# Batch 0 of a fused RWKV, routed attention and MLP kernel: projected and scaled in two halves of three chunks, with the instruction order derived anew

## Chip, cores, metric

One Trainium2 chip, one core of it. The metric is device time in microseconds of one execution. Five engines matter: TensorE (PE in the rows; PEld is its weight load), VectorE (DVE), ScalarE (ACT), GpSimd (POOL) and SyncE (SP), which issues all DMA transfers.

## What is computed

The reference, cut to what matters (B=4 batches, H=8 heads, S=768 tokens, D=48, so 384 model columns; E=4 experts of width 64; hidden width 1536):

```
for t in range(S):                       # RWKV, per batch and head
    cur = einsum('bhd,bhe->bhde', u * k[t], v[t])
    y[t] = einsum('bhd,bhde->bhe', r[t], state + cur)
    state = w[t] * state + einsum('bhd,bhe->bhde', k[t], v[t])
x = y as [B, S, 384]
w = softmax of the top 2 of x @ w_gate   # per token
for e in range(E):                       # causal attention of each expert
    q, k, v = x @ wq[e], x @ wk[e], x @ wv[e]
    ye = softmax(causal(q k^T / 8)) @ v @ wo[e]
    out += (w of e where e is chosen) * ye
xn = layernorm(out) * g_ln
return out + relu(xn @ w1) @ w2
```

## The kernel before

A batch is 6 chunks of 128 tokens. `rwkv_chunk` (24 times) does the recurrence of a chunk with two scans on VectorE (L637 backward, L649 forward), masked products `pa` and `py` on TensorE, and adds the chunk's 384 columns to the tile `xf` (`xsum`, L782); ScalarE's `xabs` (L786) leaves the sum of the absolute values of each row in `xm`.

`project(b)` waits for all six `xabs`, takes the largest row sum (L803), turns it into a power-of-two scale (`pow2_scale`, L395 to L428, with two hops over TensorE), and splits `xf` into a high and a low fp16 half (`xs`, L823 and L827). SyncE transposes each chunk (L836). TensorE makes queries and keys (`pq`, L858: four column blocks `mt`, each in two halves of three chunks) and values (`pv`, L913, one per chunk). Queries and keys go through ScalarE and VectorE (`qk`, L871, L877) and are stacked by 4 or 6 DMAs per `mt` into `qs`, `kd` and `low` (L894 to L897). The gate weights of all six chunks follow in `g_rank`, `g_exp`, `g_norm`.

`attend(b)` goes through 6 row blocks i and 4 experts e: scores `ps` (L1000 to L1002), their smallest negated value on VectorE (`s_max`, L1012), the exponential and its high half on ScalarE (L1020, L1029), the low half on VectorE (`s_lo`, L1034), a DMA transpose into `pt` (`s_tr`, L1042), then the product with the values, `po` (L1055). After four experts the block is normalized, transposed (L1096) and projected, `px` (L1107). Two blocks make a group: `norm` (its last VectorE step is `n_lo`, L1165, then a transpose, L1172) and `mlp`: 108 matmuls `pm` (L1200) and 72 `pz` (L1233). There are 12 groups.

The weights w1 and w2 are also loaded, repacked (L491 to L493), scaled and split in the kernel, in its first 200 us.

Every step is recorded as an operation with its engine, a cost, what it waits for and which buffers it takes and frees. `Plan.order` sorts the operations: of those that can start about now on an engine, the one with the smallest due number goes first. The due numbers come from the table `PLACE` (by group and by step). So the order of each engine is fixed when the program is built, and each engine works strictly in that order. Where the planner sees TensorE free before 208 us of its own count, it puts in a `spin` (L583), a matmul into a scratch bank whose result nobody reads.

At the end `f_rows` (L1328) makes a flag from bounds on the data; only if it fails is everything computed again by a general loop.

Of the kernel before, what the change touches and what calls it, by code (L numbers as in the profile page):

```python
# [9 lines left out]
F32 = mybir.dt.float32  # L10
# [280 lines left out]
def transpose_time(cols):  # L291
    return 1.2 + 0.05 + max(0, cols - 768) * 0.28e-3, (0.9, cols * 1.17e-3)


def copy_time(elems, n=1):
    return 0.43 * n, (0.43 * n + 0.45, P * elems * 4 / 360e3)
# [1119 lines left out]
```

## Time and profile before

| | us |
|---|---|
| median of 3 runs | 718.54 |
| lowest, highest | 717.99, 721.35 |
| the profiled execution | 721.46 |
| its span, first to last instruction | 719.3 |
| TensorE busy | 661.2 |
| VectorE busy | 518.3 |
| ScalarE busy | 397.0 |
| mean granted TensorE clock | 0.964 |

2.2 us of the profiled execution lie outside its span. TensorE's busy time includes the spins, which do nothing for the output. Busy times overlap between engines; what counts is which engine is the last to be ready in each stage.

### The profile page before, as it was taken

Reading aid. Unit: us, or ns where it says so; the run is one execution under the profiler, and the core shown is the slowest. Engines: PE = TensorE matmul, PEld = TensorE weight load, DVE = VectorE, ACT = ScalarE, POOL = GpSimd, SP = SyncE. Lnnn points to the kernel's source line nnn. Section 1 sums busy time; section 2 is a strip of 40 time slices with the busy share of each in tenths; the row PEclk is TensorE's granted clock in tenths of the full one; section 3 lists DMA queues with packets and bytes.
Section 4 is the critical chain, followed back from the end, with each engine's and each line's share of the span. In section 5 each row is a group of like instructions: output and inputs, shape, how many; then the busy total and the mean of one; then the engine's idle time right before and its main releaser. Section 6 shows DMA issues by size and latency. Waiting matters only on the chain.

```text
span 719.3 us, 15287 instructions
## 1 busy us (share of the span) xinstructions
PE 661.2 (92%) x5651; PEld 478.4 (67%) x5656; DVE 518.3 (72%) x1300; ACT 397.0 (55%) x1175; POOL 95.9 (13%) x118
## 2 busy tenths in 40 slices
PE   7799668998999999988999899999999899999996
PEld 4467325666686787767678777758676667776773
DVE  8889989988899887787889857755554566564321
ACT  4634387756766655546766554656552467554410
POOL 4311200221323122102032200000000000000000
PEclk9989769999999999998999999999999999999998
DMA  8365664665859867647759434575445335444210
GB/s 301 117 197 177 222 171 103 165 163 106 165 152 228 132 144 184 183 86 154 152 122 235 121 86 85 107 119 93 92 64 118 71 60 118 90 81 75 43 45 26
DMA packets 172275, 92.59 MB, mean 129 GB/s; under 512 B 144416, under 2 KB 156448, under 8 KB 172192
## 3 DMA queue, kind: packets, MB, share of 16 engines
q1 hardware_dynamic: 172192, 91.53, 56.1%
q8 instruction: 46, 0.75, 0.5%
q14 instruction: 37, 0.30, 0.1%
HBM read 44.31 MB, written 4.72 MB: 68 GB/s over the span
## 4 chain that ended last, share of the span: by engine, by line
PE 59%; DMA 20%; DVE 14%; issue 2%; ACT 2%; SPq 1%; POOL 1%; DVEq 0%; ACTq 0%; POOLq 0%
PE pz L1233 16%; DMA pt<-hl 14%; PE pm L1200 13%; PE pq L858 4%; PE py L753 4%; PE po L1055 4%; PE spin L583 3%; PE pv L913 3%; PE pa L713 3%; PE px L1107 2%; PE pd L762 2%; PE ps L1000 2%; DVE bw L637 2%; PE ps L1001 2%; DVE w_w L492 1%
## 5 line engine op out<-in xcount | busy, mean ns | idle before, releaser
L1200 PE MATMUL pm<-xnT,w_w 128*128 128x256 f16 x1296 | 155.5, 274 | 0.5 <-DVE hid L1215 0.3
L1233 PE MATMUL pz<-w_w,hid 128*128 128x384 f16 x864 | 151.8, 326 | 0.2
L1200 PEld LDWEIGHTS <-w_w 128*128 128x128 f16 x1296 | 124.1, 98 | 17.0 <-DVE hid L1215 1.0
L1233 PEld LDWEIGHTS <-hid 128*128 128x128 f16 x864 | 81.5, 98 | 49.1 <-issue 0.7
L1020 ACT ACTIVATE ps<-ps,bias,scales 128x512 f32<-128x512 f32 (+3 forms) x128 | 76.6, 599 | 62.8 <-DVE junk L1012 62.3
L583 PE MATMUL spin<-starts,ident 128*128 128x512 bf16 x293 | 79.3, 412 | 2.9 <-POOL ident masks.py:199 2.1
L1034 DVE SCALAR_TENSOR_TENSOR hl<-ps,hl 128x512 f16<-128x512 f32 (+3 forms) x128 | 60.4, 499 | 24.6 <-ACT hl L1029 24.2
L1012 DVE TENSOR_SCALAR_CACHE_REDUCE junk<-ps,scales 128x512 bf16<-128x512 f32 (+3 forms) x96 | 58.8, 613 | 24.0 <-PE ps L1002 12.2
L1215 DVE SCALAR_TENSOR_TENSOR hid<-pm,hid 128x512 f16<-128x512 f32 x72 | 49.3, 686 | 28.5 <-ACT hid L1211 28.4
L1211 ACT ACTIVATE hid<-pm 128x512 f16<-128x512 f32 x72 | 42.6, 593 | 45.2 <-PE pm L1200 44.9
L1055 PE MATMUL po<-vt,pt 128*128 128x64 f16 x1008 | 45.2, 194 | 20.8 <-DMA pt<-hl 20.4
L1029 ACT ACTIVATE hl<-ps 128x512 f16<-128x512 f32 (+3 forms) x128 | 52.8, 448 | 20.0 <-DMA pt<-hl 19.5
L1055 PEld LDWEIGHTS <-pt 128*128 128x128 f16 x1008 | 38.9, 99 | 35.2 <-DMA pt<-hl 30.9
L583 PEld LDWEIGHTS <-ident 128*128 128x128 bf16 x298 | 30.3, 105 | 38.1 <-issue 13.1
L858 PE MATMUL pq<-xT,w_qk 128*128 128x384 f16 x288 | 49.6, 326 | 0.6 <-DVE inv_w L420 0.5
L753 PE MATMUL py<-seq,am 128*128 128x48 f32 x384 | 47.7, 279 | 0.0
L753 PEld LDWEIGHTS py<-seq,am 128*128 128x128 f32 x384 | 46.9, 198 | 1.1 <-DVE w_w L492 0.2
L677 POOL TENSOR_TENSOR tok<-tok 128x384 f32<-128x384 f32 x24 | 24.7, 1027 | 149.0 <-DMA tok<-in_tok_dram 137.8
L1149 POOL TENSOR_TENSOR rs_y<-rs_v,half 128x2 f32<-128x2 f32 x12 | 9.1, 760 | 262.8 <-DVE rs_v L1145 262.7
L1000 PE MATMUL ps<-kd,qs 128*128 128x512 f16 (+3 forms) x128 | 39.3, 308 | 2.3 <-DVE hl L1034 2.0
L697 POOL TENSOR_TENSOR cv<-seq,cb 128x384 f32<-128x384 f32 x24 | 23.4, 976 | 130.7 <-ACT cv L786 45.9
L858 PEld LDWEIGHTS <-w_qk 128*128 128x128 f16 x288 | 27.8, 98 | 19.1 <-DVE lg L926 0.6
(183 smaller groups left out, 1092.5 us busy)
## 6 DMA issues: line engine op xcount, KB each, us to landing
seq<-in_seq_dram SPq DMA_DIRECT2D x48, 256.0 KB, 4.4
tok<-in_tok_dram SPq DMA_DIRECT2D x24, 384.0 KB, 3.7
w_raw<-in_w_dram SPq DMA_DIRECT2D x24, 384.0 KB, 4.0
seq<-in_seq_dram SPq DMA_DIRECT2D x24, 258.5 KB, 2.9
seq<-in_seq_dram SPq DMA_DIRECT2D x24, 192.0 KB, 4.6
out_dram<-x SPq DMA_DIRECT2D x24, 192.0 KB, 2.2
qs<-qk SPq DMA_DIRECT2D x32, 96.0 KB, 2.3
kd<-qk SPq DMA_DIRECT2D x32, 96.0 KB, 2.2
```

The source lines that it names most:

```text
L583: T.matmul(bank("m", "spin"), ident16, ballast, start=True, stop=True)
L753: T.matmul(t["py"][:, h * D : (h + 1) * D], ams[h % 2][:, h // 2, :], t["vt"][:, h * D : (h + 1) * D], start=(c == 0 and h == 0), stop=(h ...
L858: T.matmul(h["pq", half][:, :384].rearrange("p (c t) -> p c t", t=P), wt["qk"][:, lw, kk, mt * P : (mt + 1) * P], t["xT"][:, 3 * half : 3 ...
L1000: T.matmul(ps, q, t["kd"][:, e, k0:k1], start=True, stop=False)
L1012: V.tensor_scalar(junk[:, k0:k1], h["ps"][ip], t["nesc"], least[:, :1] if ip else 3.0e38, op0=OP.mult, op1=OP.min, accum_out=h["bias"])
L1020: A.activation(ps, ps, AF.Exp, bias=h["bias"], scale=t["esc"], accum_out=r["sums"][:, ip, e : e + 1])
L1029: A.activation(h["hl"][:, k0:k1], ps, AF.Copy, scale=2.0 ** 14)
L1034: V.scalar_tensor_tensor(out=h["hl"][:, W + k0 : W + k1], in0=ps, scalar=2.0 ** 14, in1=h["hl"][:, k0:k1], op0=OP.mult, op1=OP.subtract)
L1055: T.matmul(r["po"][:, e * HD : (e + 1) * HD], r["pt"][e][:, lp * (i + 1) + kb, :], t["vt"][:, kb, lv, e * HD : (e + 1) * HD], start=(e == ...
L1200: T.matmul(h["pm"][:, j * 256 : (j + 1) * 256].rearrange("p (c t) -> p c t", t=P), wt["w1"][:, 4 * kk + f // 3, lw, f % 3 * P : (f % 3 + 1 ...
L1215: V.scalar_tensor_tensor(out=hid[fp][:, 1], in0=h["pm"], scalar=0.0, in1=hid[fp][:, 0], op0=OP.max, op1=OP.subtract)
L1233: T.matmul(h["po"][:, :DM], hid[fp][:, lh, c0 : c0 + P], wt["w2"][:, 2 * fp + j, lw, :], start=(fp + j + i == 0), stop=(fp == NF // 2 - 1 ...
```

## The change

Six things, by the diff.

1. Batch 0 alone (`SPLIT = 1`) is projected in two parts, chunks 0 to 2 and 3 to 5. Its scale waits for three `xabs` and is taken from the first half with a target of 2^10 in place of 2^14. Each `x_hi` now also waits for its chunk's own sum.
2. In that batch `pq` is done half by half, and each half of an `mt` has its own buffer and its own 4 or 6 stacking DMAs, of 384 columns instead of 768: 40 DMAs instead of 20.
3. The scores of row blocks 0 to 2 of batch 0 wait only for the first four stacks and the first three values; the gate steps are done once per half.
4. The flag checks in addition that the second half stays below 2^15 times under that scale (three small VectorE steps).
5. Five small products of scales move from GpSimd to VectorE.
6. `PLACE` holds other numbers, the planner's costs of DMAs and of some steps are other, and the `pt` transposes of a batch must keep their recorded order. `junk`, which nobody reads, shrinks to 512 columns.

```diff
-    ('av', 0, 0): -11321.78, ('av', 0, 1): -5901.15, ('av', 0, 2): -17242.11, ('av', 0, 3): -12213.17,
+    ('av', 0, 0): -16394.28, ('av', 0, 1): -10556.83, ('av', 0, 2): -24769.79, ('av', 0, 3): -11565.63,
...
+SPLIT = 1
...
-    return 1.2 + 0.05 + max(0, cols - 768) * 0.28e-3, (0.9, cols * 1.17e-3)
+    return 1.2 + 0.05 + max(0, cols - 768) * 0.28e-3, (0.9, cols * 1.2e-3)
...
-    return 0.43 * n, (0.43 * n + 0.45, P * elems * 4 / 360e3)
+    return 0.43 * n, (0.43 * n + 0.92, P * elems * 4 / 335e3)
...
-    junk = const.tile([P, S], BF16, name="junk")
+    junk = const.tile([P, 512], BF16, name="junk")
...
-        G.tensor_tensor(out=t[:, 0:1], in0=inv[:, 0:1], in1=inv[:, 1:2], op=OP.mult)
+        V.tensor_tensor(out=t[:, 0:1], in0=inv[:, 0:1], in1=inv[:, 1:2], op=OP.mult)
...
-                G.tensor_scalar(wt["gs"], g_sb, s, None, op0=OP.mult)
+                V.tensor_scalar(wt["gs"], g_sb, s, None, op0=OP.mult)
...
+        split = b < SPLIT
+        parts = ((0, 1, 2), (3, 4, 5)) if split else (tuple(range(NC)),)
...
-            V.tensor_reduce(out=cm, in_=xf[b][1], axis=AX.X, op=OP.max)
+            V.tensor_reduce(out=cm, in_=xf[b][1][:, : len(parts[0])], axis=AX.X, op=OP.max)
...
-        scaled = pow2_scale(x_max, 1, 14, f"x{b}", x_scales, [chunk[NC * b + c]["xabs"] for c in range(NC) if b < B] + small_done[:1])
+        scaled = pow2_scale(x_max, 1, 10 if split else 14, f"x{b}", x_scales,
+                            [chunk[NC * b + c]["xabs"] for c in parts[0] if b < B] + small_done[:1])
...
-            @op("A", 0.61, after=[scaled], take=[("xs", (b, c))])
+            @op("A", 0.61, after=[scaled] + ([chunk[NC * b + c]["xsum"]] if split else []), take=[("xs", (b, c))])
...
-        for mt in range(4):
+        for mt, half in [(mt, half) for half in range(2) for mt in range(4)] if split else [(mt, half) for mt in range(4) for half in range(2)]:
...
+            hlk = ("hl", ("q", b, mt, half if split else 0))
+            first, last = split or half == 0, split or half == 1
...
-                    nc.sync.dma_start(dst[a, e, :], hi[a, :])
+                    nc.sync.dma_start(dst[a, e, cols], hi[a, :])
...
+        for some in parts:
+            gate, n, cs = {}, len(some), slice(some[0], some[-1] + 1)
...
-                @op("PE", (2 * W + P) / 2400 + 0.0025 * (2 * npc + 1), after=pr["stacks"], follow=[before_ps, pr["mv"][-1]], take=aks, free=final)
+                @op("PE", (2 * W + P) / 2400 + 0.0025 * (2 * npc + 1), after=pr["stacks"][:4] if pr["split"] and i < 3 else pr["stacks"], follow=[before_ps, pr["mv"][2 if pr["split"] and i < 3 else -1]], take=aks, free=final)
...
-                @op("SP", d, after=[s_lo], dma=lat, take=[("pt", key)], free=[("hl", key)])
+                @op("SP", d, after=[s_lo], follow=me["tr"][-1:], dma=lat, take=[("pt", key)], free=[("hl", key)])
...
+            V.tensor_reduce(out=ok[:, k], in_=xf[b][1][:, 3:], axis=AX.X, op=OP.max)
+            V.tensor_tensor(out=ok[:, k], in0=ok[:, k], in1=cur[b]["s"], op=OP.mult)
+            V.tensor_scalar(ok[:, 1:2], ok[:, k], 2.0 ** 15, ok[:, 1:2], op0=OP.is_le, op1=OP.mult)
```

What moves, at three places. First VectorE where batch 0's scale begins, with the row `xcm` (its reduction). `xf`'s row names the chunk by the middle number of `py_5` or `py_2`; `w_w` is the repacking of w1 and w2. Before:

```order
L782 TENSOR_TENSOR xf_315<-py_5_941,cv_5_1017 128x384
L420 TENSOR_SCALAR inv_w_1035<-sc_w_1019 128x1
L422 TENSOR_SCALAR inv_w_1035<-inv_w_1035 128x1
L423 TENSOR_SCALAR inv_w_1035<-inv_w_1035 128x1
L424 TENSOR_SCALAR inv_w_1035<-inv_w_1035 128x1
L428 RECIPROCAL s_w_1036<-inv_w_1035 128x1
L803 TENSOR_REDUCE xcm_1046<-xm_316 128x1
L491 TENSOR_SCALAR w_w_127<-w_raw_1003 128x384
```

and now:

```order
L786 TENSOR_TENSOR xf_319<-py_2_568,cv_2_618 128x384
L677 TENSOR_TENSOR rp_3_632<-seq_3_420,fw_3_614 128x512
L495 TENSOR_SCALAR w_w_126<-w_raw_474 128x384
...
L724 COPY_PREDICATED am_91<-above,pa_3_0_673 128x512
L724 COPY_PREDICATED am_92<-above,pa_3_1_674 128x512
L814 TENSOR_REDUCE xcm_704<-xm_320 128x1
L779 TENSOR_TENSOR dec_98<-dec_98,pd_3_696 48x4x48 x2
L641 SCALAR_TENSOR_TENSOR bw_4_716<-seq_4_625,starts 128x516
```

The scale's reduction stood behind chunk 5 and w1's scale; it now stands in chunk 3, before the scan of chunk 4.

Second TensorE at the first matmul of the first MLP group (`pm_0_0`). `ps_4_0` is the score of row block 4, expert 0; `pd_4` and `pa_4` belong to chunk 4 of batch 1. Before:

```order
L762 MATMUL pd_4_2523<-seq_4_2071,k2t_4_2506 112x96 x4
L1000 LDWEIGHTS qs_1439
L1000 MATMUL ps_4_0_0_2531<-kd_1566,qs_1439 128x512
L1001 LDWEIGHTS qs_1439
L1001 MATMUL ps_4_0_0_2531<-low,qs_1439 128x512
...
L1002 MATMUL ps_4_0_512_2532<-neg,ident_73 128x128
L1200 LDWEIGHTS w_w_126
L1200 MATMUL pm_0_0_2543<-xnT_0_2478,w_w_126 128x256
```

and now:

```order
L717 MATMUL pa_4_0_2414<-rp_4_2396,k_1_4_2345 128x128
L717 MATMUL pa_4_1_2415<-rp_4_2396,k_1_4_2345 128x128
L1027 LDWEIGHTS qs_1014
L1027 MATMUL ps_3_0_0_2436<-kd_1124,qs_1014 128x512
L1028 LDWEIGHTS qs_1014
L1028 MATMUL ps_3_0_0_2436<-low,qs_1014 128x512
L1029 LDWEIGHTS ident_73
L1029 MATMUL ps_3_0_0_2436<-neg,ident_73 128x128
L1228 LDWEIGHTS w_w_126
L1228 MATMUL pm_0_0_2444<-xnT_0_2371,w_w_126 128x256
```

The first MLP group used to start behind the first score of block 4; it now starts behind the first score of block 3, and three scores of block 3 and the `py` of chunk 4 come after it.

Third TensorE between the last score of row block 4 (`ps_4_3`) and the product that uses it (`po` with `pt_4_3`), in batch 0. Before:

```order
L1002 MATMUL ps_4_3_512_2943<-neg,ident_73 128x128
...
L1233 MATMUL pz_0_0_2927<-w_w_127,hid_0_3_2719 128x384
...
L1055 MATMUL po_4_2726<-vt_1213,pt_4_2_2940 128x64
...
L1233 MATMUL pz_0_1_3033<-w_w_127,hid_0_0_2603 128x384
...
L1002 MATMUL ps_5_0_512_3044<-neg,ident_73 128x128
...
L1233 MATMUL pz_0_1_3033<-w_w_127,hid_0_3_2719 128x384
...
L1055 MATMUL po_4_2726<-vt_1213,pt_4_3_3041 128x64
```

and now:

```order
L1029 MATMUL ps_4_3_512_2952<-neg,ident_73 128x128
...
L1261 MATMUL pz_0_1_2982<-w_w_127,hid_0_0_2489 128x384
...
L1083 MATMUL po_4_2788<-vt_914,pt_4_2_2949 128x64
...
L1029 MATMUL ps_5_0_512_3027<-neg,ident_73 128x128
...
L735 MATMUL pk_0_3057<-ident,k_2_0_3003 128x128 x4
...
L1261 MATMUL pz_0_1_2982<-w_w_127,hid_0_2_2589 128x384
...
L1083 MATMUL po_4_2788<-vt_914,pt_4_3_3024 128x64
```

Between the two stood 54 matmuls `pz`; now 18 `pz` and the `pa` and `pk` of one chunk stand there.

## Rows read from the trace of the kernel before

**Rows 1.** The page's first line: span and instructions.

```profile
span 719.3 us, 15287 instructions
```

**Rows 2.** Busy time by stage: start:end, length, PE, PEld, DVE, ACT, POOL, PEclk, DMA, GB/s.

```profile
0.00:192.90 192.90, 162.68 (x1094) 104.23 (x1100) 173.01 (x396) 112.13 (x373) 43.72 (x56) 0.90 0.64 173
192.90:224.00 31.10, 30.47 (x320) 26.12 (x321) 27.26 (x67) 20.43 (x64) 10.94 (x11) 1.00 0.64 170
224.00:282.00 58.00, 55.37 (x515) 41.22 (x514) 48.33 (x109) 36.06 (x115) 11.05 (x12) 1.00 0.79 164
```

**Rows 3.** Waits of TensorE from 200 us on: total us, times, longest.

```profile
PE po L1055 <- DMA pt<-hl: 18.1, 18, 2.5
```

**Rows 4.** Timeline at the first MLP group: start, us, instructions [idle before <-releaser].

```profile
193.79 0.96 DVE L1165 TENSOR_TENSOR x<-xn,x 128x768 f16<-128x768 f32 x1 [1.33 <-ACT x L1161]
...
198.51 1.70 PE L1200 MATMUL pm<-xnT,w_w 128*128 128x256 f16 x14 [0.18 <-DMA xnT<-x]
```

**Rows 5.** Groups by line on VectorE: count | busy us, mean ns | idle before.

```profile
L1012 DVE TENSOR_SCALAR_CACHE_REDUCE junk<-ps,scales 128x512 bf16<-128x512 f32 x48 | 35.8, 746 | 17.5 <-PE ps L1001 9.2 <-PE ps L1002 7.0
L720 DVE COPY_PREDICATED am<-above,pa 128x512 f32<-128x512 int8 x48 | 32.9, 721 | 1.4 <-PE pa L713 1.3
L1034 DVE SCALAR_TENSOR_TENSOR hl<-ps,hl 128x512 f16<-128x512 f32 x48 | 32.5, 682 | 14.0 <-ACT hl L1029 13.9
L637 DVE TENSOR_TENSOR_SCAN bw<-seq,starts 128x516 f32<-128x516 f32 x24 | 30.9, 1288 | 3.9 <-DMA seq<-in_seq_dram 3.9
L649 DVE TENSOR_TENSOR_SCAN fw<-seq,begin 128x516 f32<-128x516 f32 x24 | 30.4, 1268 | 0.0
L673 DVE TENSOR_TENSOR rp<-seq,fw 128x512 f32<-128x512 f32 x24 | 16.3, 680 | 0.0
L782 DVE TENSOR_TENSOR xf<-py,cv 128x384 f32<-128x384 f32 x24 | 13.1, 548 | 3.1 <-PE py L753 2.8
L924 DVE SCALAR_TENSOR_TENSOR vt<-pv,vt 128x256 f16<-128x256 f32 x24 | 10.1, 420 | 9.4 <-ACT vt L920 9.3
L926 DVE TENSOR_SCALAR lg<-pv,scales 128x4 f32<-128x4 f32 x24 | 5.1, 211 | 0.0
```

**Rows 6.** Pieces of the chain that ended last, 200 to 480 us: start, us, work.

```profile
204.06 1.06 PE py L744 x8
...
212.06 1.72 PE py L753 x16
...
214.75 1.09 PE pa L713 x16
...
220.36 0.84 PE pd L762 x8
...
346.05 0.35 PE po L1055 x12
```

**Rows 7.** Timeline from the last score of block 4 to the second group.

```profile
224.21 0.38 PE L1000 MATMUL ps<-kd,qs 128*128 128x512 f16 x1 [0.66 <-DVE hl L1034]
...
224.43 0.38 PE L1001 MATMUL ps<-low,qs 128*128 128x512 f16 x1
...
224.81 3.09 PE L1233 MATMUL pz<-w_w,hid 128*128 128x384 f16 x18
...
224.87 0.95 DVE L1165 TENSOR_TENSOR x<-xn,x 128x768 f16<-128x768 f32 x1
...
236.64 0.61 PE L1055 MATMUL po<-vt,pt 128*128 128x64 f16 x15 [0.98 <-DMA pt<-hl]
...
239.75 2.46 PE L1200 MATMUL pm<-xnT,w_w 128*128 128x256 f16 x21
```

**Rows 8.** DMA issues by line: count, KB each, median us to landing.

```profile
qs<-qk SPq DMA_DIRECT2D x32, 96.0 KB, 2.3
```

**Rows 9.** The stacking DMAs on SyncE: ns shortest/median/longest, first and last start.

```profile
L894 SPq DMA_DIRECT2D qs<-qk x16: 461/588/607, 125.3 to 549.0; - x16
```

**Rows 10.** Waits of SyncE's own queue, 60 to 200 us: total us, times, longest.

```profile
SPq L516 <- ACT w_raw L387: 23.7, 14, 4.7
```

More of the change, by code (lines that the diff above doesn't have):

```diff
@@ L96 @@
+    'q_lo': -1695.12, 's_exp': 4159.27, 's_hi': -8021.02, 's_lo': -1628.8, 's_max': -1264.05, 's_tr': -7263.35,
+    'scan': -1954.79, 'se': 777.16, 'stack': -456.7, 'state': 1790.61, 'times': 1101.35, 'top': 1748.4,
+    'unpack': -2317.52, 'v_hi': -2981.92, 'v_lo': -54.31, 'vc': 384.67, 'w_check': -1553.81, 'ws_hi': 2581.74,
+    'ws_lo': -4721.06, 'ws_load': 4770.08, 'ws_top': -11817.48, 'x_hi': 1855.08, 'x_lo': 8338.9, 'x_tr': 8850.16,
+    'xabs': -8510.13, 'xsum': -2993.07,
 }
@@ L717, in rwkv_chunk @@
         for j in range(2):
-            @op("V", 0.69, after=[mm_a], follow=[me["am"] if j else before.get("am")], take=[mine("am", j)], free=[mine(ta, j)])
+            @op("V", 0.72, after=[mm_a], follow=[me["am"] if j else before.get("am")], take=[mine("am", j)], free=[mine(ta, j)])
             def am_copy(j=j):
@@ new lines, in project, with mm_q @@
+            hlk = ("hl", ("q", b, mt, half if split else 0))
+            first, last = split or half == 0, split or half == 1
+            if first:
+                los = []
+                h = {}
+            at("proj", 3 * half, mt=mt)
+            ak = ("a", ("q", b, mt, half))
+            mms = []
+            for kk in range(KK):
+                @op("PE", 0.49, after=xT_done[3 * half : 3 * half + 3] + small_done, follow=[mms[-1] if mms else mm_before] + prev.get("s", [])[-1:],
+                    take=[] if kk else [ak], free=[("xT", b)])
+                def mm_q(kk=kk, mt=mt, half=half, h=h):
+                    if kk == 0:
+                        h["pq", half] = bank("a", f"pq_{b}_{mt}_{half}")
+                    for i, (lw, lx) in enumerate(passes):
+                        T.matmul(h["pq", half][:, :384].rearrange("p (c t) -> p c t", t=P),
+                                 wt["qk"][:, lw, kk, mt * P : (mt + 1) * P],
+                                 t["xT"][:, 3 * half : 3 * half + 3, lx * KK + kk, :],
+                                 start=(kk + i == 0), stop=(kk == KK - 1 and i == 2))
+                mms.append(mm_q)
@@ new lines, in project, with q_hi @@
+            mm_before = mms[-1]
+            cols = slice(half * 384, (half + 1) * 384)
+            @op("A", 0.49, after=mms, follow=[prev.get("l", [None])[-1], hi_before], take=[hlk] if first else [])
+            def q_hi(half=half, mt=mt, h=h, cols=cols, first=first):
+                if first:
+                    h["hl"] = buf("hl", [P, 2, S], F16, f"qk_{b}_{mt}_{half}")
+                A.activation(h["hl"][:, 0, cols], h["pq", half][:, :384], AF.Copy, scale=2.0 ** -15)
+            hi_before = q_hi
@@ new lines, in q_lo @@
+            @op("V", 0.56, after=[q_hi], follow=[lo_before], free=[ak])
+            def q_lo(half=half, h=h, cols=cols):
+                V.scalar_tensor_tensor(out=h["hl"][:, 1, cols], in0=h["pq", half][:, :384], scalar=2.0 ** -15,
+                                       in1=h["hl"][:, 0, cols], op0=OP.mult, op1=OP.subtract)
+            lo_before = q_lo
+            los.append(q_lo)
+            if not last:
+                continue
+            if not split:
+                cols = slice(0, S)
@@ L883, in stack @@
             @op("SP", 2.5 if mt < 2 else 3.7, after=los, follow=stacks[-1:], dma=(2.5, 1.0) if mt < 2 else (3.7, 1.4), free=[hlk],
[L884 to L886 removed]
+                take=([("qs", b)] if mt == 0 else [("kd", b), ("kl", b)]) if m == 0 and (half == 0 or not split) else [])
+            def stack(mt=mt, m=m, h=h, cols=cols):
+                if mt == 0 and "qs" not in t:
@@ L967, in project @@
         cur[b] = t
-        proj[b] = dict(stacks=stacks, v=vdone, mv=mvs, gate=g_norm)
+        proj[b] = dict(stacks=stacks, v=vdone, mv=mvs, gates=gates, split=split)
     blk = {}
@@ L1325 @@
     kept = {}
-    @op("V", 1.0, pair=True, after=[me["check"] for me in chunk])
+    @op("V", 1.0, pair=True, after=[me["check"] for me in chunk] + [me["xabs"] for me in chunk[: NC * SPLIT]])
     def f_rows():
```

168 lines of the change are left out of this document (69 added, 99 removed), and 78 rows, old and new, of the table PLACE.

## Prediction

> **What bounds the kernel now.** I read the busy time by stage first [rows 2]. Up to 192.9 us VectorE is busy 173.0 us of 192.9, 90%, with few waits; TensorE shows 162.7, but that includes the spins, which do nothing. So VectorE sets the pace of this stage: it carries the recurrence of two batches, the repacking of w1 and w2 and batch 0's attention. From 192.9 us on TensorE is busy 30.5 of 31.1 and 55.4 of 58.0 at a granted clock of 1.00, without spins, and VectorE has some room (27.3 and 48.3). So the kernel has two parts: one in which VectorE's list has to be worked off, and one in which TensorE's has.
>
> The timeline then shows where they meet [rows 4]: the last VectorE step of the first normalization, `n_lo`, starts at 193.8, and the first matmul `pm` of the first MLP group at 198.5, 4.7 us later, after an idle TensorE of 0.18 us. From there the waits of TensorE are mostly of one kind [rows 3]: `po` for the transposed `pt`, 18.1 us in 18 waits. The time is therefore about: when VectorE is through with what stands ahead of the first `n_lo`, plus what TensorE still has to do then, plus the waits for `pt`.
>
> **The change part by part.** *VectorE ahead of the first `n_lo`.* I counted its rows in both orders. Ahead of it now stand 12 instead of 16 of `s_max` (the four of row block 3 come later), 12 instead of 15 of `s_lo`, 20 instead of 22 mask copies, one backward and one forward scan less, one `rp` and one `xsum` less, and two value tiles less. By the means [rows 5] that is 4 x 0.746 = 2.98, 3 x 0.682 = 2.05, 2 x 0.721 = 1.44, 1.29, 1.27, 0.68, 0.55 and 2 x (0.420 + 0.211) = 1.26, in all 11.5 us. The five products of scales that leave GpSimd cost VectorE five small steps; the nearest row, a 128x4 product, is 0.211, so 1.06 us. That leaves 10.5 us. VectorE took 192.9 / 173.0 = 1.115 us of time for a busy one [rows 2], so `n_lo` comes 10.5 x 1.115 = 11.7 us earlier (10.5 if its waits stay as long as they are; I take 11.7, since the stage is one of full use). The order shows how this is possible: the scale's reduction stood behind chunk 5 and now stands in chunk 3, so projection and attention of the first half run beside chunks 3 to 5 and the repacking.
>
> *TensorE behind that point.* What was done ahead of the first `pm` and now comes after it: three `po` of 0.35 (36 matmuls), a chunk's two kinds of `py` of 1.72 and 1.06, its `pd` of 0.84 [rows 6], and eight 128x512 score matmuls of 0.22, from the distance of two starts [rows 7], 1.76. Sum 1.05 + 1.72 + 1.06 + 0.84 + 1.76 = 6.4 us. So the gain at this point is 11.7 - 6.4 = 5.3 us.
>
> *Does it last?* At the first matmul of the second group both TensorE lists hold the same work, and VectorE's list ahead of the second `n_lo` is only about 1 us shorter than before: the lead is spent there. But VectorE does not bind at that point: `n_lo` starts at 224.87 and the group's first `pm` at 239.75 [rows 7], 14.9 us later, where the first group needed 4.7 [rows 4]. Some 10 us of slack cover it. So I let the 5.3 us last.
>
> *Edits that I cost at nothing.* The gate steps are done twice for batch 0, some 13 steps more of about 0.2 us; half of them stand behind the first `n_lo`, where VectorE has room. Without that cover they cost 2.6 us. The three steps of the flag stand in the last third, where VectorE is half idle; at most 0.6 us. The smaller `junk` changes no instruction's size. The planner's new costs act only through the order. The recorded order of the `pt` transposes binds SyncE, which issues them one at a time anyway; what is queued behind a late one is loads and other transposes, and `po` waits for them. I cannot see such a wait in the trace of before; its bound is the longest wait for `pt` now, 2.5 us [rows 3], on either side, since another order can also remove one.
>
> *The 20 further DMAs.* Each takes SyncE 0.588 us [rows 9], together 11.8 us between the start of the projection and the first MLP group. In that stage SyncE often waits itself, for example 23.7 us for w_raw's buffers alone [rows 10], so I take zero, with 11.8 as the upper bound. A half could land sooner than the 2.3 us of a whole [rows 8]; the row does not show a half, so I take no gain.
>
> [...] The whole transfers have 96 KB, the halves would have 48. [...]
>
> *Sum.* The profiled execution is 721.5 us, its span 719.3 [rows 1]; with 5.3 less it would be 716.2. It lies 2.9 above the median of the three runs, 718.5, and the comparison is of medians: 718.5 - 5.3 = 713.2, so **713 us**.
>
> **Rivals.** *More is gained.* The 6.4 us of deferred TensorE work need not cost anything if they fill waits for `pt`, of which there are 18.1 us [rows 3]. For it: the new order puts scores of row block 3 among the first `pm`, so they run ahead of their `po`. Against it: those waits lie in 18 places up to the end, and the deferred work is placed in one. Time 718.5 - 11.7 = 706.8. Chance 0.14.
>
> *The gain is given back at the next hand-overs.* VectorE has to do the deferred work between the first and the second `n_lo`, where it is busy 27.3 of 31.1 already [rows 2], while the order gives `pt` less cover. Third place of the order: between the last score of row block 4 and its `po` stood 54 `pz`, now 18. In the trace this hand-over runs from 224.4 to 236.6 and still has 0.98 us of waiting [rows 7]. 36 `pz` at 3.09 / 18 = 0.17 are 6.2 us; the `pa` put there fills 1.09 [rows 6]. If the hand-over takes as long as before, TensorE waits 5.1 us more: 713.2 + 5.1 = 718.3. For it: the rows. Against it: the new order may leave VectorE freer at this moment, and one wait covers the next. Chance 0.26.
>
> *Slower: SyncE's queue.* SyncE works strictly in order. If it has no slack in the projection of batch 0, the 20 issues delay the transposes and weight loads queued behind them by 11.8 us [rows 9], and with them the repacking on VectorE and the first MLP group: 718.5 - 5.3 + 11.8 = 725.0. It decides once more than about half of the issue time falls on a waiting chain. For it: a projected half must pass a ring of two buffers, and the stacks of `mt` 3, second half, now stand directly ahead of the first group. Against it: SyncE's own waits [rows 10]. Chance 0.15.
>
> [...]
>
> *The change doesn't do what it says.* If the second half overflowed the scale, the flag would fail and all batches would be computed again, several hundred us. Row sums of the second half would have to be more than 16 times those of the first; the decay (0.8 to 0.95 a token) has forgotten the start within a chunk, so I give it less than 0.01 and leave it out of the range.
>
> **How the numbers follow.** About 0.5%, 3.6 us, is what a measurement of this kernel can tell from no change: below 714.9 is faster, above 722.1 slower. The forecast has 0.45 and a range of its own of 709 to 717 (from 10.5 and 11.7 on the one hand, the 2.6 us of gate steps and a wait of 2.5 on the other). Faster: 0.32 of the forecast's 0.45, all 0.14, and 0.04 of the second rival, 0.50. Within: 0.13, 0.19 and 0.01, 0.33. Slower: 0.14 of the third and 0.03 of the second rival, 0.17. The range takes in the first rival with the bound of its waits and most of the second: 704 to 723, leaving out most of the third and little at the low end.
>
> **What would show it.** Right: the first `n_lo` starts near 182 us and the first `pm` near 187; VectorE's busy share up to there stays near 90%; the second group's first `pm` stands near 234 to 236; TensorE's waits for `pt` stay near 18 us. The forecast is wrong if the first `n_lo` comes later than 188 (then see SyncE's queue and VectorE's waits before it), or if it is early and the second group still starts at 239 or later with longer waits of `po` in 190 to 260 us (the hand-overs), or if the time goes with a lower granted clock after 200 us, which no step here foresees.

## The result and the profile after

The changed kernel takes 712.43 us (median of 9 runs, 706.82 to 718.69), the kernel before, run beside it, 719.92 us (median of 9, 716.68 to 722.72). The ratio is 0.990, 95% interval 0.986 to 0.994, so it is faster by about 7.5 us. The forecast was 713.0 us. Here and below, single runs over 1.5% above the fastest of their kernel, as one of these nine (718.69), are left out of ratios and comparisons. The time is as forecast; the way to it, as the rest of this part shows, is not.

In the experiments below the changed kernel was run once more; its ratio was 0.991 (0.987 to 0.994).

The page's first line and the busy times by stage, for the changed kernel, with the columns and the stretches of [rows 1] and [rows 2]:

```profile
span 710.7 us, 15383 instructions
```

```profile
0.00:192.90 192.90, 169.91 (x1080) 110.97 (x1081) 168.86 (x387) 108.29 (x365) 43.20 (x52) 0.88 0.62 169
192.90:224.00 31.10, 31.10 (x325) 25.88 (x324) 26.38 (x71) 21.59 (x61) 6.45 (x7) 1.00 0.54 133
224.00:282.00 58.00, 51.97 (x490) 40.03 (x489) 53.75 (x125) 34.47 (x115) 14.27 (x13) 0.97 0.83 184
```

The span is 8.6 us shorter. In the first stage VectorE (third busy time) does less than before, 168.9 us against 173.0, and in the third more, 53.8 against 48.3: work was indeed moved behind the first normalization. But its share of the first stage is 88%, not the 90% on which the factor 1.115 of the forecast rested, and the granted clock there (third number from the right) is 0.88 instead of 0.90.

TensorE's waits from 200 us on, as in [rows 3]:

```profile
PE po L1083 <- DMA pt<-hl: 12.1, 14, 1.5
PE pz L1261 <- DVE x L1268: 2.1, 1, 2.1
```

The waits of `po` for `pt` went from 18.1 to 12.1 us, the longest from 2.5 to 1.5. The forecast had let them stay. The second line is new.

The timeline at the first and second MLP group, as in [rows 4] and [rows 7] (start, us, instruction):

```profile
186.18 1.75 DVE L1193 TENSOR_TENSOR x<-xn,x 128x768 f16<-128x768 f32 x1
...
192.92 1.15 PE L1228 MATMUL pm<-xnT,w_w 128*128 128x256 f16 x9
...
229.14 0.94 DVE L1193 TENSOR_TENSOR x<-xn,x 128x768 f16<-128x768 f32 x1
...
243.48 1.69 PE L1228 MATMUL pm<-xnT,w_w 128*128 128x256 f16 x14
```

The first `n_lo` is 7.6 us earlier than before (193.79), the first `pm` 5.6 us (198.51); the second `n_lo` is 4.3 us later (224.87), and so is the second group's first `pm`, by 3.7 us (239.75). At that `pm` both TensorE lists hold the same work. So in this execution the lead of the halves is not only smaller than forecast: it is gone after one group. Followed from group to group in the same way, the third group's first `pm` stands at 322.4 us instead of 317.5 (later), the seventh's at 509.8 instead of 515.9 (earlier), the last `pz` at 705.1 instead of 713.1. At the third and at the seventh group the lists hold the same work on TensorE, and on VectorE but for a step or two. The gain therefore seems to arise between the third and the seventh group, in batches 1 and 2, where no step of the forecast looked.

### The profile page after: what moved, and what is told of

The parts are those of the page before. It is cut to its first block, busy times and chain, and to the rows that moved or that the text cites. A ratio compares the mean times of both kernels' runs of the same rounds, so it can differ in the third digit from the quotient of the medians.

```text
span 710.7 us, 15383 instructions
## 1 busy us (share of the span) xinstructions
PE 664.6 (94%) x5664; PEld 486.3 (68%) x5664; DVE 523.5 (74%) x1321; ACT 397.6 (56%) x1176; POOL 95.6 (13%) x113
## 4 chain that ended last, share of the span: by engine, by line
PE 63%; DMA 17%; DVE 14%; issue 2%; ACT 1%; SPq 1%; POOL 1%; DVEq 0%; ACTq 0%
PE pz L1261 17%; PE pm L1228 16%; DMA pt<-hl 13%; PE pq L874 5%; PE po L1083 4%; PE py L757 3%; PE spin L587 3%; PE pv L933 3%; PE px L1135 2%; PE pa L717 2%; PE ps L1027 2%; PE pd L766 2%; PE ps L1028 2%; PE py L748 2%; DVE w_w L496 1%
## 5 line engine op out<-in xcount | busy, mean ns | idle before, releaser
L1261 PE MATMUL pz<-w_w,hid 128*128 128x384 f16 x864 | 153.6, 327 | 2.1 <-DVE x L1268 2.1
L587 PE MATMUL spin<-starts,ident 128*128 128x512 bf16 x306 | 81.3, 405 | 2.5 <-POOL ident masks.py:199 2.1
L757 PE MATMUL py<-seq,am 128*128 128x48 f32 x384 | 50.6, 288 | 0.5 <-DVE am L724 0.5
L757 PEld LDWEIGHTS py<-seq,am 128*128 128x128 f32 x384 | 49.6, 207 | 1.8 <-DVE am L724 0.8
L681 POOL TENSOR_TENSOR tok<-tok 128x384 f32<-128x384 f32 x24 | 28.3, 1179 | 113.4 <-DMA tok<-in_tok_dram 113.4
```

The costliest lines, as they stand in the source:

```text
L587: T.matmul(bank("m", "spin"), ident16, ballast, start=True, stop=True)
L757: T.matmul(t["py"][:, h * D : (h + 1) * D], ams[h % 2][:, h // 2, :], t["vt"][:, h * D : (h + 1) * D], start=(c == 0 and h == 0), stop=(h ...
L1261: T.matmul(h["po"][:, :DM], hid[fp][:, lh, c0 : c0 + P], wt["w2"][:, 2 * fp + j, lw, :], start=(fp + j + i == 0), stop=(fp == NF // 2 - 1 ...
```

## The experiments

Three theories stood at the beginning. **L**: the lead of the halves lasts (the forecast). **S**: the gain arises behind the third group, by itself. **Q**: what counts is VectorE's whole list ahead of some late hand-over and TensorE's behind it. To tell them apart, the order that the planner finds was written into the kernel as a list of steps and played back, so that one stretch can be taken from one kernel's order and the next from the other's:

```diff
     def order(self, look, late, warm=None):
+        if warm:
+            out = []
+            for k in map(int, ORDER.split()):
+                for _ in range(-k):
+                    x = _Op()
+                    x.run = warm["run"]
+                    out.append(x)
+                if k >= 0:
+                    out.append(self.ops[k])
...
+            return out
```

A number is a step, a negative one so many spins. The list stands ahead of the program, so line numbers are higher in the profiles of these kernels. In the short diffs below a line is a stretch of that list, or a step of it.

### Cut at the third or the seventh group

```diff
 kernel before (no halves), steps up to the first pm of group 3: its order
-steps from there on: its order
+steps from there on: the order of the change
```

> The kernel before (no halves, its own code), with its own order up to the first pm of the third MLP group (317.5 us in its profile, 322.4 in that of the change) and the order of the change from there to the end. At that point both TensorE lists hold the same work, and the VectorE lists differ by less than 1 us. Theory L, the step of the prediction (the lead won by the halves at the first normalization lasts to the end): nothing is won here, about the time of the kernel before, ratio 1.00. Theory S (the gain arises behind that point, by itself): 317.5 + (710.7 - 322.4) = 705.8 us of span, 13.5 less than before, ratio 0.981. Theory Q (the time is set by the VectorE work ahead of a late hand-over plus the TensorE work behind it, whatever came first): the time of the change, ratio 0.990.

Measured: 710.84 us, ratio 0.986 (0.981 to 0.991). A kernel without halves, without the products on VectorE, without the 20 further DMAs, has the whole gain.

```diff
 changed kernel (halves), steps up to the first pm of group 3: its order
-steps from there on: its order
+steps from there on: the order of the kernel before
```

> The changed kernel (halves) with its own order up to the first pm of the third MLP group and the order of the kernel before behind it. Theory L (a lead from the halves lasts): keeps the gain, ratio 0.990. Theory S (the gain arises behind that point): 322.4 + (719.3 - 317.5) = 724.2 us of span, 4.9 more than before, ratio 1.007. Theory Q (VectorE work ahead of a late hand-over plus TensorE work behind it): the time of the kernel before, ratio 1.00.

Measured: 723.55 us, ratio 1.009 (1.004 to 1.014). With the halves and the new order of the head alone the kernel is slower than before. L expected 1.00 for the first experiment and 0.990 for the second: it falls twice. Q expected 0.990 and 1.00, and falls with the second. S expected 0.981 and 1.007; it has both signs and about the sizes. The profile of the first experiment is of the slowest of its runs (716.5 us), that of the second of the fastest (719.0 us).

```diff
 changed kernel, steps up to the first pm of group 7: its order
-steps from there on: its order
+steps from there on: the order of the kernel before
```

> The changed kernel with its own order up to the first pm of the seventh MLP group (509.8 us in its profile, 515.9 in that of before), where all lists of both orders hold the same work, and the order of the kernel before behind it. Theory S: 509.8 + (719.3 - 515.9) = 713.2 us of span, 2.5 more than the change, ratio 0.992 to 0.994. Theory Q with the deciding hand-over in batch 1: the time of the change, 0.990, since only what comes before the seventh group counts. If the gain arose in the last third: 1.00.

Measured: 712.06 us, ratio 0.988 (0.984 to 0.992). The last third adds nothing; S had expected a small loss here, 0.992 to 0.994, and misses it.

One execution differs from the next by several us, so I read the same points in every profile that has the same list up to there: five with the old head (before, the first experiment, and three below) and five with the new one (the change twice, the second and third experiment, and one below). Means of the times in the timelines, us:

| | old | new | new less old |
|---|---|---|---|
| first `n_lo` | 192.8 (190.4 to 196.0) | 183.9 (180.0 to 187.6) | -8.9 |
| first `pm` | 198.1 (195.1 to 200.7) | 190.8 (186.8 to 194.3) | -7.3 |
| second group's `pm` | 239.4 (236.0 to 242.4) | 241.4 (237.6 to 244.8) | +2.0 |
| third group's `pm` | 318.1 (314.9 to 319.8) | 320.1 (315.8 to 323.4) | +2.0 |
| third to seventh group | 198.0 (197.6, 198.4) | 189.8 (187.4 to 192.9, four) | -8.2 |
| seventh group to last `pz` | 195.3 (three) | 195.0 (four) | -0.3 |

The three parts sum to +2.0 - 8.2 - 0.3 = -6.5 us, of the 7.5 measured. The two rows in which the ranges do not overlap near the start are the first two; the difference of 2 us at the second and third group is within the scatter of one execution.

### Where between the third and the seventh group

The busy times of that stretch, of the kernel before and of the change:

```profile
317.50:515.90 198.40, 187.22 (x1738) 140.66 (x1733) 144.76 (x388) 118.62 (x339) 20.99 (x26) 0.98 0.61 125
```

```profile
322.40:509.80 187.40, 181.93 (x1733) 139.35 (x1731) 145.77 (x393) 119.65 (x341) 21.09 (x26) 1.00 0.64 128
```

and of the first two experiments (old head and new rest, then new head and old rest):

```profile
319.80:512.70 192.90, 183.47 (x1735) 140.08 (x1731) 145.26 (x389) 119.49 (x340) 20.58 (x26) 0.99 0.62 125
```

```profile
319.70:517.30 197.60, 184.93 (x1732) 139.44 (x1730) 146.02 (x392) 118.45 (x340) 21.23 (x26) 0.99 0.63 125
```

VectorE has the same to do in all four, 145 to 146 us. Of the 11.0 us between the first two, TensorE was idle 11.2 us in the one and 5.5 in the other, and busy 5.3 us longer for the same work at a granted clock of 0.98 instead of 1.00. Its waits for `pt` in this stretch, before and in the change:

```profile
PE po L1055 <- DMA pt<-hl: 9.5, 9, 2.1
```

```profile
PE po L1083 <- DMA pt<-hl: 4.8, 6, 1.5
```

In the means of the table's executions the split is 4.8 us of idle time and 3.4 of busy time. These two profiles show the waits at their furthest apart: the first and third experiments and the second execution of the change, with the new order, have 7.1, 6.0 and 6.1 us of them, and the second experiment, with the old one, 9.5. The longer busy time goes in part with the clock: a clock of 0.98 instead of 1.00 over 198.4 us is worth about 4 us of the 5.3 (an estimate from these rows), and in the kernel before it was low, 0.82 and 0.89, from 329 to 353 us. So about half of it is waiting saved; the other half is matmul time, for which the clock accounts in part. Where a hand-over gains is seen best at the longest one, of the third expert of batch 1's last row block. The timeline before, from the row maxima (`s_max`, L1012) to the `po` that waits; SPq is SyncE's queue:

```profile
393.96 0.75 DVE L1012 TENSOR_SCALAR_CACHE_REDUCE junk<-ps,scales 128x512 bf16<-128x512 f32 x1
...
397.34 0.86 ACT L1029 ACTIVATE hl<-ps 128x512 f16<-128x512 f32 x2
398.33 0.53 DVE L782 TENSOR_TENSOR xf<-py,cv 128x384 f32<-128x384 f32 x1
...
398.77 0.68 DVE L673 TENSOR_TENSOR rp<-seq,fw 128x512 f32<-128x512 f32 x1
...
399.37 0.69 DVE L668 TENSOR_TENSOR k<-seq,bw 128x512 f32<-128x512 f32 x1
...
399.98 1.02 DVE L1034 SCALAR_TENSOR_TENSOR hl<-ps,hl 128x512 f16<-128x512 f32 x2
...
401.02 1.44 SPq L1042 DMA_TRANSPOSE pt<-hl  x1
...
406.47 0.70 PE L1055 MATMUL po<-vt,pt 128*128 128x64 f16 x18 [2.05 <-DMA pt<-hl]
```

and in the change:

```profile
391.98 0.75 DVE L1039 TENSOR_SCALAR_CACHE_REDUCE junk<-ps,scales 128x512 bf16<-128x512 f32 x1 [0.94 <-PE ps L1028]
...
393.33 0.61 DVE L1268 SCALAR_TENSOR_TENSOR x<-pz,iout,x 128x384 f32<-128x384 f32 x1
...
394.76 0.86 ACT L1056 ACTIVATE hl<-ps 128x512 f16<-128x512 f32 x2
395.38 1.02 DVE L1061 SCALAR_TENSOR_TENSOR hl<-ps,hl 128x512 f16<-128x512 f32 x2 [1.44 <-ACT hl L1056]
...
396.48 1.43 SPq L1069 DMA_TRANSPOSE pt<-hl  x1
...
400.97 0.69 PE L1083 MATMUL po<-vt,pt 128*128 128x64 f16 x18
```

Before, three steps of the recurrence (`xf`, `rp`, `k`) stand on VectorE between `s_max` and `s_lo` (and others further up); `s_hi` (the `hl` of ScalarE) is done at 398.2, but `s_lo` starts at 399.98. From `s_max` to `s_lo` it is 6.0 us. In the change VectorE has little to do there and waits for ScalarE instead, and it is 3.4 us. Not all of the difference is VectorE's, though. The transpose itself, from issue to landing, took 1.4 us less, as the two traces show for this one transpose, before and in the change:

```profile
DMA to landing us min/median/max: 5.4/5.4/5.4
```

```profile
DMA to landing us min/median/max: 4.0/4.0/4.0
```

Over all transposes between the third and the seventh group the mean landing is the same (3.5 and 3.6 us), so this part belongs to the single hand-over. The new order puts the recurrence of batch 3 later and MLP work earlier, so batch 1's hand-overs seem to have VectorE more to themselves.

Two more cuts ask whether the gain is made at each hand-over where it stands (theory W) or by the mixture further back (theory T):

```diff
 kernel before, steps up to the first pm of group 4 (in the second run: group 5): its order
-steps from there on: its order
+steps from there on: the order of the change
```

> The kernel before with its own order up to the first pm of the fourth MLP group (374.6 us in its profile) and the order of the change behind it. The head runs gave third to seventh group: old order 198.4 and 197.6 us, new order 187.4 to 192.9. In the old order 4.7 us of po waits (1.08, 1.90, 1.00 and 0.75) and a granted clock of 0.82 and 0.89 over 24 us stand between the third and the fourth group, 3.2 us of po waits (2.05 and 1.12) between the fourth and the fifth. Theory W (the gain is the sum of what each hand-over saves, where it stands): about half of the gain is left, third to seventh group 193 to 195, ratio 0.993 to 0.997. Theory T (the gain is made by the mixture of MLP and recurrence behind the fourth group, and the earlier waits only anticipate it): all of it, ratio 0.986 to 0.990.

Measured: 716.69 us, ratio 0.996 (0.994 to 0.999); third to seventh group 194.8 us, `po` waits in it 7.8 us. About half of the gain is left: W. (The profile is of the fastest of its runs, 711.7 us.)

> The same with the old order up to the first pm of the fifth MLP group (446.9 us in the profile of before). Theory W: nearly nothing of the gain is left, third to seventh group 196 to 198, ratio 0.998 to 1.002. Theory T with the deciding mixture between the fourth and the fifth group: nothing left either; with the mixture behind the fifth: 0.986 to 0.990.

Measured: 732.32 us, ratio 1.017 (1.013 to 1.021). Nothing is left, which both theories allowed, but it is also 11 us slower than before, outside the range of either. The stretch and its waits:

```profile
318.80:529.60 210.80, 192.07 (x1736) 142.79 (x1733) 145.61 (x389) 119.75 (x339) 22.18 (x26) 0.96 0.57 115
```

```profile
PE po L1182 <- DMA pt<-hl: 12.2, 9, 2.3
PE ps L1127 <- DVE hl L1161: 5.1, 5, 1.6
```

The second line, scores waiting for a bank that `s_lo` (`hl`) gives back, is 0.6 us in the kernel before. The orders differ most at the fifth group: the old one starts it at 446.9 us, the new one at 406.8. Pasted together there, batch 2's attention seems to lack the MLP work that had covered it in the new order and has already been spent in the old. A seam between two orders can thus cost time by itself. In the second experiment none is seen: from the third to the seventh group it takes 197.6 us, the kernel before 198.4.

Two more runs tried to name the part of the mixture that matters:

```diff
 kernel before: its order throughout, but
-steps of chunks 18 to 23 (and the flag) where they stand
+steps of chunks 18 to 23 (and the flag) behind the neighbour that each has in the order of the change
```

> The kernel before with its own order throughout, but with every step of batch 3's recurrence (chunks 18 to 23, on all engines and with their loads) and of the flag behind the third group moved to the neighbours that they have in the order of the change: the pa of chunks 21, 22 and 23 then stand at 439 to 480 us instead of 390 to 416. Theory R (the gain behind the third group comes from spreading this VectorE-heavy recurrence over 320 to 500 us, so that the pt hand-overs of batch 1 wait less): third to seventh group 187 to 193 us instead of 198.4, waits of po in it near 5 instead of 9.7, ratio 0.985 to 0.990. Rival (the gain is a matter of the fine order at each hand-over): little of it, ratio 0.997 to 1.003.

```diff
 changed kernel: its order throughout, but
-steps of chunks 18 to 23 (and the flag) where they stand
+steps of chunks 18 to 23 (and the flag) behind the neighbour that each has in the order of the kernel before
```

> The changed kernel with its own order, but with the steps of batch 3's recurrence and of the flag behind the third group moved to the neighbours that they have in the order of the kernel before (the pa of chunks 21 to 23 some 30 to 60 us earlier). Theory R (the gain comes from spreading this recurrence): the gain goes, third to seventh group 195 to 200 us instead of 187.4, waits of po in it 9 or more, ratio 0.998 to 1.01. Rival (fine order at each hand-over): most of the gain stays, ratio 0.988 to 0.994.

Measured: 779.51 us, ratio 1.082 (1.077 to 1.088), and 766.92 us, ratio 1.067 (1.063 to 1.070). Both are 47 to 67 us slower than either kernel, and both expectations fail. In the first, three waits of 9.8 to 10.9 us make up over half of the added idle time of TensorE, as two lines of its waits between the third and the seventh group show:

```profile
PE pm L1326 <- DVE hid L1341: 21.2, 3, 10.2
PE ps L1126 <- DVE hl L1160: 14.8, 6, 10.9
```

Single steps seem to have come to stand ahead of others on which a whole queue hung. The runs therefore do not answer their question. That the recurrence's place in batches 1 and 2 is the part that matters stays an inference from the timelines above; shown is only that moving it alone, in this way, costs 47 us or more. Nor does any run separate the engines: each stretch that was played back holds the order of all of them, SyncE's transposes included.

### The clock in the recurrence of batch 0

In the profile of the change TensorE idles from 34.0 to 40.2 us, ahead of chunk 2's `pa`. Busy time and granted clock (PEclk, third column from the right) right behind:

```profile
36.00:42.00 6.00, 1.81 (x16) 1.78 (x16) 5.45 (x14) 1.38 (x5) 0.00 (x0) 0.62 0.38 80
42.00:48.00 6.00, 6.00 (x30) 5.38 (x26) 5.39 (x8) 1.17 (x5) 1.29 (x1) 0.50 0.58 184
48.00:54.00 6.00, 6.00 (x23) 3.79 (x23) 3.07 (x7) 2.68 (x14) 1.99 (x2) 0.50 0.37 113
```

At a clock of 0.50 the 16 `pa` of chunk 2 (40.19 us) take 2.08 us and its 8 `pd` (49.00 us) 1.77; at 1.00 the next 16 `pa` (56.30 us) take 1.16 and the next 8 `pd` (58.35 us) 0.95. VectorE is busy 3.07 of 6 us in the last row, and its idle time from 36 to 60 us is put down to TensorE:

```profile
L724 DVE COPY_PREDICATED am<-above,pa 128x512 f32<-128x512 int8 x4 | 2.7, 721 | 4.0 <-PE pa L717 4.0
L779 DVE TENSOR_TENSOR dec<-dec,pd 48x192 f32<-48x192 f32 x4 | 1.4, 352 | 3.6 <-PE pd L766 3.6
```

So the stage that the forecast took to be VectorE's is, for a while, TensorE's, at a granted clock of 0.50. The experiment fills the idle time with spins:

```diff
+spin, 24 times
 mm_a (chunk 2)
...
+spin, 9 times
 mm_a (chunk 4)
```

> The changed kernel with 33 more spins: 24 ahead of chunk 2's pa (idle from 34.0 to 40.2 us) and 9 ahead of chunk 4's (idle from 63.9 to 66.8); every other instruction in its place. Theory C (TensorE's low granted clock between 36 and 60 us, 0.50 to 0.62, holds the recurrence, and VectorE loses about 6.7 us there waiting for pa and pd): granted clock near 1.0 there, VectorE busy over 5.5 of each 6 us, first n_lo near 180 to 182 instead of 186.2. If such a lead lasts, 706 to 709 us; by theory S or where a later hand-over binds, the time of the change, about 713, with the lead gone by the second or third group. Rival: VectorE's idle time there is not from the clock, and nothing moves (first n_lo at 186).

> The kernel with 33 more spins once more, beside the changed kernel on the same chip. If the clock of the recurrence's stretch is worth its 4 us at the end: 3 to 4 us below the changed kernel, ratio to before 0.985. If the head of the program is no longer what counts behind the second group: the same as the changed kernel within 1.5 us.

Measured: 709.30 us, ratio 0.985 (0.980 to 0.991), and again 709.57 us, ratio 0.984 (0.980 to 0.988). The same three rows, and the same two groups of VectorE, in the first of these runs:

```profile
36.00:42.00 6.00, 5.05 (x36) 2.74 (x35) 5.86 (x16) 1.37 (x6) 0.00 (x0) 1.00 0.33 76
42.00:48.00 6.00, 6.00 (x47) 4.76 (x47) 5.96 (x11) 1.94 (x8) 1.29 (x1) 1.00 0.67 205
48.00:54.00 6.00, 5.82 (x52) 4.61 (x50) 5.89 (x11) 3.21 (x13) 2.33 (x2) 1.00 0.49 158
```

```profile
L851 DVE COPY_PREDICATED am<-above,pa 128x512 f32<-128x512 int8 x4 | 2.7, 722 | 0.0
L906 DVE TENSOR_TENSOR dec<-dec,pd 48x192 f32<-48x192 f32 x4 | 1.4, 343 | 0.0
```

The theory of the clock holds here: the clock stays at 1.00 up to 54 us and VectorE's 7.6 us of waiting are gone. Further on it does not: in the first of these runs it is 0.72 from 54 to 60 us, and 0.58 and 0.50 from 66 to 78, in spite of the 9 spins. The first `n_lo` comes at 182.0 and 179.3 us, the mean of the change being 183.9; in the mean 3.2 of the 7.6 us arrive there. Against the means of the change nothing is left at the second group's first `pm`, 242.2 and 241.1 against 241.4, and the third group's is at 320.5 and 320.0 against 320.1; behind it the profiles show 1.5 us up to the seventh group and 1.3 from there on.

At the end the spins do pay. The second run stood beside the change on the same chip: six runs from 706.1 to 710.6 us against eleven from 710.4 to 718.6, in the mean 4.5 us less (95% interval 2.4 to 6.6). The ratios' intervals, 0.980 to 0.988 and 0.987 to 0.994, touch because both carry the spread of the kernel before. This is the first branch of the expectation, 3 to 4 us below the change, and not the second. In this one pair of profiles the lead of the spins also lasts: 244.8 against 241.1 us at the second group, 323.4 against 320.0 at the third. Which of the two pictures is typical, and what the spins change behind the third group, where the list is the same, stays open.

### Two steps at the second group

Between its first two groups the change has a place of its own where TensorE waits, in these two lines of its waits from 192.9 to 243.5 us:

```profile
PE pz L1261 <- DVE x L1268: 2.1, 1, 2.1
PE sc_x L406 <- DVE xcm L814: 1.1, 1, 1.1
```

```diff
 mk_cb (chunk 12)
+o1 (the largest value xcm, batch 1)
+m_out (x, group 1, first half)
 forth (chunk 12)
-o1 (the largest value xcm, batch 1)
 s_max (batch 0, block 4, expert 3)
 mk_rp (chunk 12)
-m_out (x, group 1, first half)
 n_lo (group 2)
```

> The changed kernel with two VectorE steps a little earlier: the largest value xcm for batch 1's scale and the first group's m_out (x) stand ahead of the forward scan of chunk 12 instead of behind it (xcm) and behind two more steps (m_out). In the profile of the change TensorE idles there for 1.07 us (sc_x) and 2.07 us (pz), and the granted clock of 216 to 234 us is 0.91. Theory H (the halves' lead at the first pm is lost between the first and second group partly at this place): idle between the two groups from 3.1 to below 1.5 us, clock near 1.0, the second group's pm 2 to 4 us earlier (240 instead of 243.5), time 709 to 711, ratio about 0.986. Rival (the lead is gone because the deferred TensorE work fills that stretch, and waits elsewhere take over): second group at 242 to 243, ratio 0.990 as the change.

Measured: 713.72 us, ratio 0.993 (0.989 to 0.996). The waits of the same stretch (188.7 to 242.1 us):

```profile
PE po L1210 <- DMA pt<-hl: 3.0, 1, 3.0
PE ps L1154 <- DVE hl L1188: 0.6, 1, 0.6
PE sc_x L544 <- DVE dg_x L540: 0.5, 1, 0.5
PE pz L1388 <- DVE x L1395: 0.3, 1, 0.3
```

Of the two waits, 3.2 us, 0.3 of `x` are left, as meant, and `sc_x` waits 0.5 for its next step. But a `po` now waits 3.0 us in their stead, and the clock from 216 to 234 us is 0.81, where Theory H had it near 1.0 (0.91 in the change). The rival holds. With the spins as well:

```diff
+spin, 24 times ahead of chunk 2's mm_a, 9 times ahead of chunk 4's
+o1 and m_out ahead of forth (chunk 12), as above
```

> The changed kernel with both: the 33 further spins of the run with more spins (which gave ratio 0.985) and the two VectorE steps earlier. If both are separate losses: second group's pm at 237 to 239, time 705 to 708, ratio 0.981. If the head of the program does not matter for what comes behind the third group: 709 to 712, ratio 0.986 to 0.990.

Measured: 712.59 us, ratio 0.990 (0.987 to 0.993): by its ratio no better than the change, and the two losses don't add up to a gain. Beside the run with the two steps alone, on the same chip, it is 1.1 us lower in the median, which the scatter does not tell from nothing; so the worth of the spins is clear on one chip only.

The change itself, beside the last runs:

> The changed kernel as it is, once more, beside the other runs of this call: ratio 0.990; first n_lo at 180 to 186 us, second group's pm at 238 to 244, third to seventh group 187 to 190 us.

Measured: 713.56 us, ratio 0.991. Its profile, with the second group's `pm` at 244.8 us and the first `n_lo` at 187.6, lies a little outside the expected ranges: one execution is a poor witness for a few us. Two versions are ahead of both kernels by the median, the one with spins (0.984 and 0.985) and the old head with the new rest (0.986). The spins are told from the change by the direct comparison above; the old head was not run beside the change, and its interval overlaps.

## Why the forecast was right in its number and wrong in its reason

*VectorE ahead of the first `n_lo`: the work right, the time three quarters in size.* The forecast was 11.7 us earlier, from 10.5 us less work times 1.115. The profile shows 7.6, the mean of five executions 8.9. The work was counted rightly: VectorE's busy time ahead of `n_lo` fell by 10.7 us, from 173.0 to 162.3. The factor did not hold: its waits did not shrink with the work but grew from 20.8 to 23.9 us, since in the new head it also waits 7.6 us for `pa` and `pd`, with TensorE at a granted clock of 0.50 from 38 to 54 us. With the spins, where that wait is gone, `n_lo` comes at 180.7 in the mean of two, 12.1 us ahead of the old head's 192.8, about as forecast.

*TensorE behind that point: 6.4 us of deferred work, net 5.3. Mis-sized.* The `pm` was to follow `n_lo` by the 4.7 us of [rows 4]. In the new head it follows by 6.7 us (192.92 - 186.18), in the means by 6.9. The lead at the first `pm` is 7.3 us, and less the 6.4 of deferred work 0.9 is left instead of 5.3. The deferred work itself was about rightly sized: from the first `pm` to the second group's, TensorE's matmuls take 46.8 us instead of 39.0, and 0.9 of the 7.8 goes with a lower clock (0.97 there in the profile of the change, 1.00 before).

*"So I let the 5.3 us last." This is the step that failed.* At the second group, with the same work on TensorE, the new head is not 5.3 us earlier but, in the means, 2.0 later; the ranges overlap, so a loss is not shown by the profiles, but the forecast lead is absent. Summed over TensorE's instructions of the traces up to there (idle, spins, other matmuls; means of five executions each), the old head takes 32.4 + 74.2 + 132.7 us, the new one 25.9 + 74.9 + 140.6. The halves do take 6.5 us of idle time away. But the same matmuls take 7.9 us longer. Most of it stands ahead of the first `pm`: there they take 93.8 us, as in the old head (93.7), although 6.4 us of work has gone behind it. The granted clock is the visible difference. From 36 to 72 us, before and in the change:

```profile
36.00:72.00 36.00, 34.28 (x231) 23.91 (x233) 32.19 (x60) 13.52 (x51) 6.17 (x6) 0.91 0.60 187
```

```profile
36.00:72.00 36.00, 27.68 (x156) 21.34 (x156) 27.77 (x63) 11.02 (x42) 8.34 (x6) 0.66 0.42 124
```

Taking from each matmul's time the share of the clock that was not granted while it ran, up to the second group 6.3 us are lost in the old head and 15.0 in the new (means of five). This estimate, 8.7 us more, covers the 7.9. It is not an experiment: the spins with which the clock was higher (0.88 instead of 0.66 from 36 to 72 us) take TensorE's time themselves. Slack between `n_lo` and `pm`, on which the forecast relied [rows 7], is no reserve where TensorE's own list fills it.

The experiments say the same without a profile: halves with the old rest 1.009, no halves with the new rest 0.986.

*"The `pt` waits stay near 18 us", and the order costed at nothing within 2.5 us. Wrong, and this is where the gain is.* They fell to 12.1, and between the third and the seventh group from 9.5 to 4.8, with the granted clock from 0.98 to 1.00; that stretch is 8.2 us shorter in the means. The forecast counted the new order only up to the second group. A table of order numbers that is derived anew moves the whole program, and [rows 3] had shown that the waits lie in 18 places up to the end.

*The rivals.* "Given back at the next hand-overs" came true as far as the lead goes, by another mechanism: between the first two groups of the change TensorE waits for `xcm` and `x`, and no `po` waits. Its time of 718.3 us was nevertheless not reached, because of the gain behind. "More is gained" counted on the waits for `pt`, and of these the deferred work did fill the 1.6 us that stand between the first two groups of the kernel before; but idle time there as a whole went from 2.3 to 3.7 us in the means, and the other waits that fell lie where no deferred work stands. "SyncE's queue" did not decide: the first `n_lo` is earlier and not later. Its premise on the halves held: on SyncE the issue of one takes as long as that of a whole (`qs` from 60 to 200 us, medians 0.567 us now and 0.567 and 0.569 before). So did the forecast's, that they land no sooner. The stacking DMAs of the change, as in [rows 8], whole ones and halves:

```profile
qs<-qk SPq DMA_DIRECT2D x24, 96.0 KB, 3.0
kd<-qk SPq DMA_DIRECT2D x24, 96.0 KB, 2.2
...
qs<-qk SPq DMA_DIRECT2D x16, 48.0 KB, 3.0
kd<-qk SPq DMA_DIRECT2D x16, 48.0 KB, 3.0
```

The halves all lie in batch 0. In that stage of the kernel before (60 to 200 us) the wholes landed in 3.3 (`qs`) and 2.2 us (`kd`), the halves of the change in 3.0 and 3.0: here half the bytes landed no sooner, taken together. The double number of issues shows no cost at the first `n_lo`; SyncE had waits of its own to spend [rows 10], and those for the buffers of `w_raw` went from 23.7 to 11.7 us.

The gate steps, the flag, the products on VectorE and the smaller `junk` were not tried one by one. Together with the halves and the new head they show no gain: the first experiment has none of them and stands at 0.986.

Of the signs that the forecast named, the first `n_lo` came by 188 us but not near 182 in this profile, VectorE's share up to there was 87 instead of 90%, the second group stood at 243.5 and not at 234 to 236, and the `pt` waits were 12 and not 18. By its own list the reason was wrong. The number came out by luck: a lead of 5.3 us that did not last was about as large as a gain that was not foreseen, 8.2 us behind the third group less the 2.0 ahead of it.

## What to carry to other kernels

Follow a lead from one point at which the lists hold the same work to the next, and not from one event to the next: idle time saved early is gained only if the later work takes no longer. When a change comes with a newly derived order, compare the order over the whole program, above all at the hand-overs that wait now; to find out which part pays, play back one order up to such a point and the other behind it. Compare two versions beside each other, and not through their ratios to a third: that told the spins from the change. And read a few us from several executions: with the same list, the second group started anywhere from 237.6 to 244.8 us.

## What the runs showed of the hardware

In the change TensorE did nothing from 34.0 to 40.2 us. The granted clock was 1.00 from 30 to 36 us, 0.86 from 36 to 38 and 0.50 from 38 to 54, although from 42 us on TensorE was busy 6.00 of 6 us; from 54 to 60 us it was 0.96. With 24 spins in that gap it stayed at 1.00 up to 54 us. What I had not expected is that VectorE, in a stage that its list seemed to bind, would lose 7.6 us from 36 to 60 us in waits for TensorE. Nor that repairing it brings so little at the next points: the spins themselves take TensorE's time (81.0 us of them up to the second group in the first of these runs, instead of 74.7 in the change), while idle time and the other matmuls fell by 4.6 and 2.9 us. The 4.5 us by which the kernel with spins is ahead at the end, on the chip where both ran, are not explained by that.
